# Another order of hand-placed items, and one cast of values on ScalarE instead of GpSimd

## The chip, the cores and the metric

The kernel runs on 1 core of one Trainium2 chip. Its engines are TensorE (PE, with the loading of stationary operands shown apart as PEld), VectorE (DVE), ScalarE (ACT), GpSimd (POOL) and SyncE (SP), which here only issues DMAs. The metric is the device time of one execution in microseconds; the median of several runs counts.

## The reference

Attention for 4 batches of 8 heads (768 rows, 64 wide), then a two-layer MLP with a prelu over the 3,072 rows that come out:

```python
scores = q @ k.T / 8                         # per batch and head
mask   = causal                              # heads 0, 2, 6 ("retrieval")
mask   = causal & (key < 4 | row - key < 64) # the other heads ("streaming")
a = softmax(where(mask, scores, -1e9))
x = a @ v                                    # 3072 x 512 over all heads
h = x @ w_in                                 # 512 -> 2048
g = maximum(h, 0) + alpha * minimum(h, 0)
out = g @ w_out                              # 2048 -> 512, float32
```

Inputs are float32 in DRAM; the kernel computes with bf16 operands.

## The kernel before

**Pairs.** A batch's eight heads are worked in four pairs: heads (2,6), (1,5), (0,4), (3,7). A pair has a number n = 4 * batch + place, from 0 to 15; "batch 1's first pair" is pair 4, the retrieval heads 2 and 6 of batch 1, and pair 5 holds two streaming heads.

**Items.** The whole program is cut into 1,112 named items, each a few instructions, and emitted in the order of a table of names written at the top of the file:

```python
for name in ORDER:
    if not beside_burst(name):
        emit_burst()
    I[name]()
```

Every engine executes its own instructions in that order; an instruction that waits holds up all behind it on the same engine. Waits between engines are put in by the framework. The names, with n a pair and t a tile of 256 or 512 rows:

- `Lq`, `Lk`, `Lv` load queries, keys, values of a pair as float32 (SP); `Cq`, `Ck`, `Cv` cast them to bf16 on an engine that the strings `CQ`, `CK`, `CV` name (V, A, P for DVE, ACT, POOL). `Cv` is L370, tile `vb<-raw`.
- `Tq`, `Tk` transpose on PE (L385), `tq`, `tk` copy the result out of PSUM (L390, L410 to L418).
- `S` scores (L447 or L454), `s` their exp on ACT (L493 for retrieval heads, into `eR`; L565 and L567 for streaming ones, into `eS`), `m` the mask, multiplied on DVE (L502 for `eR`, 128x128; L576 and L579 for `eS`).
- `An.h` the product with the values (L603), `an.h` its normalisation on DVE (L613, L614), which also gives its PSUM bank back; `Xn` a DMA that transposes the result into the MLP's input.
- `P`, `p`, `g` the first layer's matmuls (L649), its relu on ACT (L654) and the prelu on DVE (L661); `O`, `o` the second layer (L669) and its copy and store (L675, L679).
- For four of the eight tiles (t = 0, 2, 4, 7) the second layer is done with seven products instead of eight (Strassen's scheme): `W1` to `W4` subtract blocks of w_out from each other (L723, DVE, 128x2048), `Gt.x` add or subtract blocks of g (L728, DVE, 128x2048), `Mt.x.s` are the products (L741, PE, 8 matmuls of 256 columns each), `k` and `c` keep and combine them (L769, L776, L779 and others). For example, `M0.2` reads plain blocks of g and w_out, `M0.4` reads W4, which needs W1; `W2` also needs W1.

**Bursts of scores.** Score matmuls of pairs 4 and up are not emitted at their item: `S` collects them, and the next item that does not stand in the list of harmless ones (`beside_burst`) emits what has been collected, as one burst. If both heads have at least `SPLIT` = 576 columns in it, they are paired: each matmul uses 64 rows of the array and the two heads run side by side (L454); otherwise each uses the whole array, with zeros in the other half (L447).

```python
if min(columns) < SPLIT:
    for x in burst:
        nc.tensor.matmul(*x[3:6], start=True, stop=True)             # L447
else:
    ...
        nc.tensor.matmul(to, keys[own], queries[own], ...)           # L454
```

**Shape of the program.** Batch 0's attention comes first, then items of the attention of one batch are mixed with MLP items of the batch before. The attention of batch 1 (pairs 4 to 7) runs beside the MLP of batch 0; the first layer of batch 1's rows (tile 2, `P2.x`) begins at 80.85 us.

Of the kernel before, what the change touches and what calls it, by code (L numbers as in the profile page):

```python
# [32 lines left out]
near1 Cv4 tq7 Lk9 a5.1 Lk10 a5.0 Lq9 X5 Lk11 Cv7 m4.1.4 G0.1 G0.3 M0.1.0 M0.1.1 c0.00 G0.2 S6.1.0 S7.0.2 S6.0.3 S7.1.1
S6.0.1 S7.1.0 s6.1.0 s7.1.1 s7.1.0 A4.0 a4.0 m7.1.0 S6.0.5 s6.0.3 s6.0.1 m7.1.1 S6.0.0 O1.0.0 O1.0.1 S7.0.0 S6.1.2
s6.0.5 s6.0.0 m6.0.3 s7.0.2 m6.1.0 S6.1.1 m7.0.2 S7.1.2 m6.0.0 S6.0.4 s6.0.4 Lq8 Cv6 s6.1.1 A4.1 m6.1.1 M0.6.1 s7.1.2
S7.0.1 a4.1 s6.1.2 X4 s7.0.1 M0.6.0 m6.0.5 S6.0.2 s7.0.0 s6.0.2 m7.1.2 A7.1 k0.01 m6.1.2 m6.0.1 A6.1 m6.0.4 A6.0
m7.0.1 m7.0.0 A7.0 O1.0.2 O1.0.3 a6.1 a6.0 M0.5.0 M0.5.1 k0.11 a7.1 a7.0 W3 M0.7.1 M0.7.0 G0.4 M0.3.1 M0.3.0 c0.01 X6
X7 P2.2 Ck9 Cq9 Cq8 Lq10 P2.5 p2.5 g2.5 P2.8 p2.8 Lq11 P2.15 g2.8 p2.15 g2.15 p2.2 g2.2 P2.0 Dk8.0 Dk9.1 p2.0 g2.0
P2.6 p2.6 g2.6 c0.10 c0.11 Dk8.1 Dq8 Dk9.0 Lv10 P3.0 p3.0 P2.9 P2.4 p2.9 g2.9 g3.0 P3.12 p3.12 Dq9 Ck10 g3.12 P3.2
o1.0 p2.4 g2.4 p3.2 g3.2 Cq10 P2.14 p2.14 g2.14 P2.3 p2.3 g2.3 P2.10 p2.10 g2.10 P3.14 p3.14 g3.14 P2.7 p2.7 g2.7  # L40
P2.11 p2.11 g2.11 P2.13 Dq10 Lv8 P3.8 P3.6 p2.13 g2.13 S8.1.5 Lv11 S9.0.0 S8.1.4 p3.8 g3.8 p3.6 g3.6 S8.0.5 S8.0.1
P2.12 P3.10 Cq11 S9.1.1 s9.0.0 s8.0.5 m8.0.5 p2.12 s8.1.4 m8.1.4 m6.0.2 s9.1.1 s8.1.5 m9.0.0 m9.1.1 g2.12 Ck11 S8.0.3
s8.0.3 P2.1 p2.1 m8.1.5 Cv8 m8.0.3 p3.10 g3.10 S8.0.0 s8.0.0 P3.4 p3.4 g3.4 M2.4.0 M2.4.1 k2.10 s8.0.1 g2.1 Dk10.1
S10.1.0 m8.0.1 s10.1.0 m10.1.0 O3.0.0 O3.0.1 G2.1 G2.3 Lv9 Cv9 Dk11.0 Dq11 S9.1.0 S9.0.2 S9.0.1 S9.1.2 S10.1.2 S8.0.4
S8.1.1 s9.1.0 O3.0.2 O3.0.3 M2.2.0 M2.2.1 m8.0.0 Lq13 Lk13 s9.0.2 Dk10.0 Dk11.1 Cv10 s10.1.2 s9.0.1 S11.0.1 S11.0.0
S10.1.1 s8.0.4 s9.1.2 m9.1.2 o3.0 s8.1.1 S8.1.3 S11.0.2 s10.1.1 s8.1.3 m10.1.2 m9.0.2 m9.0.1 A9.0 k2.00 m9.1.0 A9.1
m8.0.4 m10.1.1 A10.1 M2.1.0 S8.0.2 a9.0 a9.1 s11.0.2 m11.0.2 s8.0.2 m8.1.3 X9 M2.1.1 s11.0.1 a10.1 s11.0.0 A8.0 G2.2
S10.0.1 S10.0.5 S8.1.0 S11.1.2 S10.0.2 M2.5.0 c2.00 M2.6.1 m8.1.1 s10.0.1 s11.1.2 m11.1.2 s8.1.0 S11.1.1 S10.0.3 Lq15
a8.0 S8.1.2 m11.0.0 s10.0.5 S11.1.0 S10.0.0 s10.0.2 S10.0.4 s8.1.2 Lv14 Lq12 m10.0.1 Cq13 m8.1.0 m10.0.5 s10.0.0 Cv11
Ck13 s10.0.4 m10.0.4 m11.0.1 m10.0.0 s10.0.3 m10.0.3 s11.1.0 s11.1.1 M2.5.1 A8.1 a8.1 m11.1.0 M2.6.0 A10.0 m11.1.1  # L50
a10.0 A11.0 Dk13.0 a11.0 k2.01 M2.7.0 A11.1 a11.1 k2.11 M2.7.1 G2.4 Cq12 X8 O3.1.0 O3.1.1 O3.1.2 O3.1.3 M2.3.1 M2.3.0
c2.10 c2.11 X10 X11 Lk12 P4.12 p4.12 c2.01 P5.14 P4.6 g4.12 P4.7 p4.7 g4.7 P4.8 p4.8 p5.14 g5.14 P5.10 p5.10 g5.10
g4.8 P5.0 p5.0 Ck12 Lq14 Dq12 g5.0 P5.12 p5.12 P5.2 P4.4 p4.4 p4.6 g4.4 g4.6 Cq14 Dk13.1 Cv14 P5.6 p5.6 p5.2 g5.2 o3.1
Dq13 g5.6 P5.4 P4.14 p4.14 g4.14 p5.4 g5.4 P4.1 p4.1 g4.1 P4.15 P4.3 p4.15 g4.15 g5.12 S13.1.0 s13.1.0 P4.10 P4.13
p4.13 g4.13 p4.10 g4.10 Lv15 Dk12.0 Dk12.1 P4.9 p4.9 g4.9 P4.5 p4.5 Lv12 Lk14 P4.2 p4.2 m12.0.2 g4.5 S12.0.1 g4.2
s12.0.1 P5.8 p5.8 O5.1.0 S12.1.1 g5.8 S13.1.1 p4.3 S12.0.0 g4.3 S12.0.5 S12.0.3 s12.0.3 O5.1.1 Lv13 Lk15 S12.1.5
s12.1.1 m12.1.1 Cv12 s12.1.5 S12.0.4 s12.0.4 P4.11 p4.11 m12.0.1 Dq14 Cq15 Ck14 m13.1.0 g4.11 s12.0.0 s12.0.5 m12.0.5
S12.0.2 s12.0.2 m12.0.4 m12.0.0 P4.0 p4.0 O5.1.2 O5.1.3 m12.0.3 A12.0 s13.1.1 m10.0.2 Dk14.0 Ck15 Cv13 o5.1 Dk14.1
S13.0.2 s13.0.2 O5.0.0 S13.0.0 S13.1.2 S13.0.1 g4.0 a12.0 S14.0.5 S12.1.2 O5.0.1 s13.1.2 G4.1 G4.3 S14.0.1 s14.0.5
S12.1.4 s13.0.0 m13.0.0 s13.0.1 s12.1.2 m13.0.1 S14.0.0 m13.1.2 S14.1.2 S14.1.0 s14.0.1 s14.1.0 m13.0.2 m14.1.0 O5.0.2  # L60
O5.0.3 S12.1.3 S12.1.0 S14.1.1 s14.0.0 s12.1.4 m12.1.4 s14.1.2 m14.1.2 m13.1.1 S14.0.2 S14.0.4 s14.0.4 s12.1.0 s12.1.3
o5.0 A13.0 M4.1.0 a13.0 Dk15.1 Dk15.0 A13.1 Dq15 m12.1.3 s14.0.2 a13.1 m14.0.5 Cv15 X13 m12.1.5 s14.1.1 m14.1.1 M4.5.0
M4.5.1 S14.0.3 S15.1.0 S15.0.2 S15.1.1 S15.1.2 m14.0.1 S15.0.1 s14.0.3 s15.1.2 s15.1.0 m14.0.4 M4.1.1 m14.0.3 m14.0.0
A14.1 A14.0 k4.0 m15.1.2 m12.1.0 A12.1 G4.2 M4.6.0 a14.0 s15.0.1 S15.0.0 M4.2.0 a14.1 X14 s15.0.2 m15.1.0 s15.1.1
m15.1.1 A15.1 M4.6.1 m15.0.2 s15.0.0 m15.0.0 m15.0.1 A15.0 a12.1 M4.2.1 k4.1 a15.1 a15.0 G4.4 M4.7.0 M4.7.1 k4.2
M4.3.1 M4.3.0 c4.11 M4.4.0 M4.4.1 X12 c4.10 X15 P7.4 P7.12 c4.01 P7.10 P7.0 p7.10 g7.10 p7.0 g7.0 P7.1 p7.1 g7.1 P7.9
P7.7 p7.7 g7.7 P7.3 p7.3 g7.3 p7.12 g7.12 P7.6 P7.13 p7.9 g7.9 P7.2 p7.2 g7.2 P7.14 p7.6 g7.6 p7.4 P6.4 P7.15 p7.14
g7.14 P6.0 p7.15 g7.15 p7.13 G7.3a P7.5 P6.6 p7.5 g7.5 g7.13 g7.4 G7.1b G7.2b P7.11 p7.11 g7.11 p6.6 P6.14 p6.0 g6.0
p6.14 M7.1.0 P7.8 p7.8 g6.14 g7.8 M7.1.1 p6.4 k7.0 g6.6 P6.10 P6.12 p6.10 G7.1a g6.10 P6.2 M7.2.0 P6.8 p6.8 M7.2.1
M7.5.0 M7.5.1 k7.2 c4.00 G7.2a M7.6.0 G7.4a M7.6.1 G7.4b M7.3.1 p6.12 g6.12 p6.2 g6.2 M7.3.0 g6.4 k7.1 g6.8 c7.01  # L70
O6.0.0 O6.0.1 O6.0.2 G7.3b M7.7.1 M7.7.0 c7.11 c7.00 d7.0 O6.0.3 L2 o6.0 l2 M7.4.1 M7.4.0 L1 l1 c7.10 d7.1 L0 l0
""".split()


# [1 line left out]
def kernel(  # L76
# [291 lines left out]
    def cast_v(n):  # L368
        vv = vb[n % NV]
        cast_of(CV[n])(vv[:, :, :, 0:D], vf[n % NF])  # L370
# [651 lines left out]
```

## Time and profile before

| | us |
|---|---|
| median of 3 runs | 224.33 |
| the three runs | 224.09, 224.33, 225.03 |
| profiled execution, its time | 224.55 |
| its span in the trace | 222.8 |
| PE busy | 214.1 (96%) |
| DVE busy | 181.7 (82%) |
| ACT busy | 142.3 (64%) |
| POOL busy | 44.8 (20%) |
| granted TensorE clock, mean | 0.999 |

The time of the profiled execution is longer than its span by what lies before the first and behind the last recorded instruction. A row of the timeline gives the start, the length from the first start to the last end, engine, line, operation, output and inputs, and how many instructions were joined; in brackets stand the idle time ahead and what ended it. A matmul's end is modelled, so where matmuls follow each other without a stop, the difference of two starts says more than a length. In a table of windows the columns behind the window are its length and the busy time of PE, PEld, DVE, ACT and POOL with their counts, then the clock, the share of DMA and its GB/s.

### The profile page before, as it was taken

What the parts mean: (1) busy time and instruction counts of PE and PEld (TensorE: products, weight loads), DVE (VectorE), ACT (ScalarE), POOL (GpSimd) and SP (SyncE); (2) the same over time, 40 slices, a digit from 0 to 9 for tenths busy, and PEclk for the clock granted to TensorE, in tenths of its full rate; (3) what the DMA queues carried; (4) which work ended last, traced back from release to release, by engine and by line L of the source; (5) the groups of instructions that cost most, each with busy time, mean ns of one, the idle gap of its engine ahead of it and who ended that gap; (6) DMA issues with size and microseconds to landing.
All of it is one profiled execution on the core that took longest, in us unless ns stands there. A gap on an engine that the chain in (4) does not pass through costs nothing.

```text
span 222.8 us, 5570 instructions
## 1 busy us (share of the span) xinstructions
PE 214.1 (96%) x2131; PEld 153.1 (69%) x2151; DVE 181.7 (82%) x441; ACT 142.3 (64%) x289; POOL 44.8 (20%) x88
## 2 busy tenths in 40 slices
...
GB/s 201 320 245 218 269 214 289 195 196 241 196 249 242 94 197 191 203 229 176 220 129 266 147 282 175 206 207 70 190 101 42 118 96 1 0 0 50 0 150 137
DMA packets 96155, 37.61 MB, mean 169 GB/s; under 512 B 83176, under 2 KB 94336, under 8 KB 96128
## 3 DMA queue, kind: packets, MB, share of 16 engines
q1 hardware_dynamic: 89600, 27.39, 57.8%
...
q8 instruction: 17, 0.28, 0.5%
q14 instruction: 10, 0.08, 0.1%
...
## 4 chain that ended last, share of the span: by engine, by line
PE 72%; DVE 8%; DMA 8%; SPq 5%; issue 3%; POOL 2%; ACT 0%; DVEq 0%; POOLq 0%
PE P L649 33%; PE P L741 20%; PE P L669 9%; DMA raw<-in_k_dram 8%; PE P L603 5%; PE P L454 3%; SPq L236 2%; DVE g L661 2%; PE P L688 2%; PE P L447 1%; SPq L220 1%; DVE eR L502 1%; DVE g L728 1%; DVE ws L723 1%; POOL w_in_b L835 1%
## 5 line engine op out<-in xcount | busy, mean ns | idle before, releaser
L649 PE MATMUL P<-xT,w_in_b 128*128 128x256 bf16 (+1 forms) x501 | 86.7, 325 | 0.7 <-issue 0.2
L661 DVE SCALAR_TENSOR_TENSOR g<-neg,oma,P 128x256 bf16<-128x256 f32 (+1 forms) x128 | 70.9, 608 | 17.1 <-ACT neg L654 16.3
L654 ACT ACTIVATE neg<-P 128x512 f32<-128x512 f32 x96 | 55.0, 602 | 35.9 <-PE P L649 27.2
L649 PEld LDWEIGHTS <-w_in_b 128*128 128x128 bf16 x512 | 49.5, 98 | 30.9 <-issue 0.2
L493 ACT ACTIVATE eR<-P 128x448 bf16<-128x448 f32 (+3 forms) x63 | 35.6, 623 | 6.8 <-PE P L454 2.9
L741 PEld LDWEIGHTS <-g 128*128 128x128 bf16 x368 | 34.8, 98 | 6.0 <-issue 0.4
L669 PE MATMUL P<-w_out_b,g 128*128 128x512 bf16 x103 | 25.4, 379 | 0.4
L741 PE MATMUL P<-ws,g 128*128 128x256 bf16 x192 | 23.4, 273 | 0.2 <-DVE ws L723 0.2
L565 ACT ACTIVATE eS<-P 128x352 bf16<-128x352 f32 x45 | 20.6, 481 | 4.0 <-PE P L454 2.6
L741 PE MATMUL P<-w_out_b,g 128*128 128x256 bf16 x176 | 21.8, 273 | 0.0
L614 DVE TENSOR_TENSOR xn<-P,rcp 128x448 bf16<-128x448 f32 (+1 forms) x32 | 19.0, 595 | 1.1
L669 PEld LDWEIGHTS <-g 128*128 128x128 bf16 x112 | 10.3, 98 | 10.8 <-DVE g L661 0.7
L679 POOL DMA_DIRECT2D out_dram<-ot x6 | 3.4, 562 | 55.8 <-ACT ot L675 50.1
L576 DVE TENSOR_TENSOR eS<-eS,ms_near 128x352 bf16<-128x352 bf16 x45 | 14.2, 335 | 0.1
L779 POOL DMA_DIRECT2D out_dram<-ot x8 | 5.9, 738 | 39.5 <-DVE ot L776 33.5
L728 DVE TENSOR_TENSOR g<-g 128x2048 bf16<-128x2048 bf16 x10 | 12.8, 1280 | 0.1
L502 DVE TENSOR_TENSOR eR<-eR,mr_near 128x128 bf16<-128x128 bf16 x54 | 10.9, 233 | 0.7 <-ACT eR L493 0.6
L603 PE MATMUL P<-vb,eS 128*128 128x65 bf16 x266 | 11.0, 193 | 0.3 <-DVE vb L327 0.2
L603 PEld LDWEIGHTS <-eS 128*128 128x128 bf16 x266 | 10.0, 97 | 1.8 <-issue 0.6
L447 PE MATMUL P<-qT,kT 128*128 128x176 bf16 (+7 forms) x66 | 10.1, 256 | 0.0
...
L603 PE MATMUL P<-vb,eR 128*128 128x65 bf16 x258 | 9.6, 192 | 0.1
...
## 6 DMA issues: line engine op xcount, KB each, us to landing
...
```

What stands on the lines that cost most here:

```text
L493: nc.scalar.activation(ebuf[n, hh][:, lo:hi].rearrange("p (x c) -> p x c", x=len(parts)), P[:, got[0]:got[0] + len(parts), 0:(hi - lo) // ...
L502: nc.vector.tensor_tensor(ej, ej, mr_near, op=ALU.mult)
L565: nc.scalar.activation(slots, sc[:, 0:352].rearrange("p (s c) -> p s c", c=176), AF.Exp, scale=scale)
L576: nc.vector.tensor_tensor(slots, slots, ms_near[:, 0:2, :] if m == 0 else ms_near[:, 1:3, :], op=ALU.mult)
L603: nc.tensor.matmul(pav[:, i, :], e[:, o:o + 128], vv[:, j, hh, 0:D + 1], start=(m == 0), stop=(m == len(terms) - 1))
L614: nc.vector.tensor_tensor(xn[n][:, 0:nt, D * hh:D * hh + D], pav[:, :, 0:D], rcp.to_broadcast([128, nt, D]), op=ALU.mult)
L649: nc.tensor.matmul(psg[:, w * i:w * (i + 1)], w_in_b[:, c, 128 * fb:128 * (fb + 1)], xT[:, c, o:o + w], start=(x == 0), stop=(x == 3))
L654: nc.scalar.activation(neg[t, f], bank(held["P", t, f][0]), AF.Relu, scale=-1.0)
L661: nc.vector.scalar_tensor_tensor(g_buf[TOK[t][1]][:, fb, 0:w], neg[t, f][:, c], oma[:, fb:fb + 1], bank(got[0])[:, c], op0=ALU.mult, op1=A ...
L669: nc.tensor.matmul(bank(held["O", t, s][0]), g_buf[TOK[t][1]][:, f, 128 * s:128 * (s + 1)], w_out_b[:, f, :], start=(f == 0), stop=(f == 15))
L728: nc.vector.tensor_tensor(G_SUM[t][x - 1][:, c, :], a[:, c, :], b[:, c, :], op=ALU.add if x == 1 else ALU.subtract)
L741: nc.tensor.matmul(bank(held[to, t][0])[:, 256 * s:256 * s + 256], g[:, f, 128 * s:128 * (s + 1)], w[:, f, :], start=(first and f == 0), s ...
```

## The change

Two things change, and nothing else. One letter in the string that names the engine for each pair's cast of values:

```diff
-    CV = "PPPPPPVVVVVVVVVV"
+    CV = "PPPPAPVVVVVVVVVV"
```

So `Cv4` runs on ACT; `Cv5` stays on POOL. And the table of items behind the first 310 (of 1,112) holds the same names in a new order. Its first lines:

```diff
-S5.0.1 p1.10 s5.0.1 P1.6 S4.1.4 m4.0.1 s4.0.3 near0 g1.10 S4.1.3 p1.12 S4.0.5 s4.0.5 m5.1.1 S4.0.4 s4.0.4 g1.12 m4.0.3
+S5.0.1 p1.10 s5.0.1 p1.12 S4.0.0 m4.0.1 g1.10 P1.6 S4.0.2 S4.0.5 S4.1.4 s4.0.3 g1.12 s4.0.0 m4.0.0 O1.1.0 near0 m5.0.2
...
```

What this does to the queues is seen in the instructions of an engine, one row each; `waits` names the engine or DMA queue whose semaphore is waited for. On PE, around the first product with pair 5's values (`A5.1`), before (`g_87` and `g_86` are the activations of 256-row and of 512-row tiles, `natm_84` the keys of pair 7, `vb` the cast values; repeated pairs of rows are left out):

```order
L385 MATMUL P<-ident,natm_84 128x128 [waits Activation_49]
...
L669 LDWEIGHTS g_87
L669 MATMUL P<-w_out_b,g_87 128x512 [waits DMASW2_49]
...
L741 LDWEIGHTS g_86
L741 MATMUL P<-w_out_b,g_86 128x256 [waits Activation_49]
...
L741 MATMUL P<-w_out_b,g_86 128x256 [waits DMASW3_49]
...
L603 LDWEIGHTS eS [waits Activation_49]
L603 MATMUL P<-vb,eS 128x65 [waits Pool_49]
```

and after:

```order
L669 MATMUL P<-w_out_b,g_87 128x512 [waits DMASW2_49]
...
L447 MATMUL P<-qT,kT 128x320
L385 LDWEIGHTS natm_84
L385 MATMUL P<-ident,natm_84 128x128 [waits Activation_49]
...
L603 LDWEIGHTS eS [waits Activation_49]
L603 MATMUL P<-vb,eS 128x65 [waits Pool_49]
...
L741 LDWEIGHTS g_86
L741 MATMUL P<-w_out_b,g_86 128x256 [waits DVE_49]
```

The sixteen L741 (`M0.2.0`, `M0.2.1`) stood ahead of `A5.1`, whose L603 waits for POOL's cast; now they stand behind it.

On DVE at the same place, around the weight sums `W2` and `W4` (the two L723 with `ws` as an input), before:

```order
L502 TENSOR_TENSOR eR<-eR,mr_near 128x128
L304 MEMSET eR 128x64
L502 TENSOR_TENSOR eR<-eR,mr_near 128x128 [waits Activation_49]
L502 TENSOR_TENSOR eR<-eR,mr_near 128x128 x2
L723 TENSOR_TENSOR ws<-w_out_b,ws 128x2048 [waits DMASW3_49,DMASW2_49,DVE_49]
L723 TENSOR_TENSOR ws<-w_out_b,ws 128x2048 [waits DVE_49]
L355 CAST natk_81<-raw 128x2x7x64 [waits DMAHW3_49,DMAHW2_49]
```

and after:

```order
L502 TENSOR_TENSOR eR<-eR,mr_near 128x128 [waits Activation_49] x2
L502 TENSOR_TENSOR eR<-eR,mr_near 128x128
L723 TENSOR_TENSOR ws<-w_out_b,ws 128x2048 [waits DMASW3_49,DMASW2_49,DVE_49]
L502 TENSOR_TENSOR eR<-eR,mr_near 128x128 [waits Activation_49]
L723 TENSOR_TENSOR ws<-w_out_b,ws 128x2048 [waits DVE_49]
L613 RECIPROCAL rcp<-P 128x7 [waits PE_49]
L614 TENSOR_TENSOR xn<-P,rcp 128x7x64 [waits DVE_49]
```

A mask now stands between the two sums, and a normalisation comes ahead of the cast of keys that followed them.

On ACT, where the moved cast lands, before:

```order
L336 CAST natq_80<-raw 128x2x6x64 [waits DMAHW1_49]
L769 COPY ot<-P 128x512 [waits PE_49]
L675 COPY ot<-P 128x512 [waits PE_49]
L390 COPY qT<-P 128x768 [waits PE_49]
L565 ACTIVATE eS<-P 128x2x176 [waits DVE_49,PE_49]
```

and after:

```order
L336 CAST natq_80<-raw 128x2x6x64 [waits DMAHW1_49]
L769 COPY ot<-P 128x512 [waits DVE_49,PE_49]
L675 COPY ot<-P 128x512
L370 CAST vb<-raw 128x14x64 [waits DMAHW7_49,DMAHW0_49]
L390 COPY qT<-P 128x768 [waits PE_49]
L565 ACTIVATE eS<-P 128x2x176 [waits DVE_49,PE_49]
```

`Cv4` (L370) stands between the copy of an MLP result and the copy of pair 7's transposed queries, and one `k` copy (L769) has moved behind the exp. The order of DMAs on SyncE's queue is the same row by row in both programs. The number of matmuls is the same too; how the score matmuls fall into bursts is not, and nine of them move from L447 to L454.

More of the change, by code (lines that the diff above doesn't have):

```diff
@@ L28 @@
 Lv6 S4.0.1 Cq6 m12.1.2 P0.5.0 s4.0.1 P0.5.1 P0.5.2 P1.12 m5.0.0 g1.4 S4.0.3 g0.7 p0.4 p0.5 m5.1.0 g0.4 g0.5 Cv5 P1.10
-S5.0.1 p1.10 s5.0.1 P1.6 S4.1.4 m4.0.1 s4.0.3 near0 g1.10 S4.1.3 p1.12 S4.0.5 s4.0.5 m5.1.1 S4.0.4 s4.0.4 g1.12 m4.0.3
-S4.0.0 m5.0.2 Tq6 S4.1.0 O1.1.0 p1.6 g1.6 O1.1.1 m4.0.5 p0.6 s4.1.4 g0.6 s4.0.0 s4.1.0 m5.0.1 S4.1.1 W1 s4.1.3 S4.0.2
-s4.0.2 m4.1.3 S4.1.5 s4.1.5 S4.1.2 m4.1.5 S5.1.2 s5.1.2 m5.1.2 s4.1.1 Tk6 tk6.1 m4.0.0 tk6.0 Tk7 O1.1.2 s4.1.2 tk7.1
-Lv4 ro1 m4.1.1 tq6 tk7.0 Cq7 M0.2.0 M0.2.1 k0.00 m4.0.4 A5.1 O1.1.3 o1.1 A5.0 m4.1.0 W2 W4 Ck8 M0.4.0 M0.4.1 k0.10 Tq7
@@ L33 @@
[L33 to L71, printed above, removed]
+S5.0.1 p1.10 s5.0.1 p1.12 S4.0.0 m4.0.1 g1.10 P1.6 S4.0.2 S4.0.5 S4.1.4 s4.0.3 g1.12 s4.0.0 m4.0.0 O1.1.0 near0 m5.0.2
@@ new lines @@
+p1.6 g1.6 S5.1.2 s4.0.5 s5.1.2 p0.6 S4.1.5 s4.1.5 O1.1.1 Tq6 s4.1.4 S4.1.3 m5.0.1 S4.1.0 s4.1.0 s4.1.3 Tk6 m5.1.1
+m4.0.5 S4.1.1 s4.1.1 tk6.1 m5.1.2 O1.1.2 W1 g0.6 S4.0.4 tk6.0 Tk7 s4.0.4 tk7.1 A5.1 Lv4 ro1 m4.0.3 m4.1.5 s4.0.2
+m4.1.0 m4.1.3 M0.2.0 m4.1.4 A5.0 tq6 tk7.0 Cq7 W2 m4.1.1 O1.1.3 M0.2.1 k0.00 W4 M0.4.0 M0.4.1 a5.1 Ck8 Tq7 near1
+m6.0.2 o1.1 a5.0 Cv4 tq7 Lk9 Lk10 Lq9 X5 S6.1.0 s6.1.0 m4.0.4 M0.1.0 M0.1.1 G0.1 k0.10 S7.0.0 S7.1.2 S7.0.2 S7.1.0
+S6.0.3 G0.3 G0.2 O1.0.0 s7.0.0 m7.0.0 c0.00 s7.1.0 S4.1.2 s7.1.2 m7.1.2 s7.0.2 A4.0 s6.0.3 m6.1.0 S6.0.5 a4.0 s6.0.5
@@ new lines @@
+m6.0.5 Lk11 Cv7 Lq8 Cv6 m7.1.0 S6.0.2 s6.0.2 O1.0.1 s4.1.2 S6.0.1 S6.1.1 m7.0.2 S7.1.1 S6.0.0 S6.1.2 s7.1.1 m7.1.1
+m6.0.3 s6.1.2 M0.6.0 s6.0.0 m6.1.2 m6.0.0 s6.0.1 s6.1.1 m6.1.1 S6.0.4 m6.0.1 M0.6.1 s6.0.4 S7.0.1 m6.0.4 A4.1 a4.1
+s7.0.1 m7.0.1 A6.1 a6.1 A6.0 a6.0 A7.1 a7.1 A7.0 a7.0 O1.0.2 M0.5.0 M0.5.1 G0.4 O1.0.3 k0.11 M0.3.0 k0.01 M0.3.1 W3
+M0.7.0 X4 X6 M0.7.1 X7 P2.7 P2.15 c0.01 P2.8 p2.15 P3.2 p2.8 Ck9 Cq9 Cq8 Lq10 Lq11 p2.7 c0.10 c0.11 P2.6 g2.7 Dk8.0
+g2.8 g2.15 p2.6 P3.12 p3.12 g3.12 Dk9.1 P3.8 p3.8 g2.6 g3.8 P2.14 p2.14 g2.14 P2.13 p2.13 g2.13 P2.11 p3.2 g3.2 p2.11
@@ new lines @@
+Dk8.1 o1.0 P2.5 P2.4 Dq8 Dk9.0 p2.5 g2.11 Lv10 g2.5 Dq9 Ck10 Cq10 Dq10 p2.4 P3.14 p3.14 g2.4 P3.0 P3.6 p3.0 g3.0 g3.14
+Lv8 p3.6 P2.0 p2.0 g2.0 g3.6 P2.3 p2.3 g2.3 P2.2 P2.10 p2.2 g2.2 P2.9 p2.10 g2.10 p2.9 S8.1.5 g2.9 S8.0.1 S9.0.0
+S8.0.5 S8.1.4 s8.1.4 P2.1 s8.0.1 m8.0.1 Lv11 Cq11 Ck11 p2.1 P2.12 g2.1 s9.0.0 p2.12 g2.12 s8.0.5 m8.0.5 s8.1.5 m8.1.5
+P3.10 p3.10 g3.10 P3.4 p3.4 g3.4 S9.1.0 S9.1.1 S8.0.0 S8.0.3 S9.1.2 Cv8 s9.1.2 m9.0.0 M2.4.0 M2.4.1 s9.1.1 s8.0.0
+O3.0.0 m9.1.1 k2.10 G2.1 m8.0.0 G2.3 O3.0.1 Dk10.1 S9.0.1 s8.0.3 S8.0.2 S9.0.2 S8.0.4 S10.1.2 s9.1.0 m9.1.0 S10.1.0
```

27 lines of the change are left out of this document (added).

## Prediction

> **What bounds the kernel now.** I read the page first (parts 1 and 4), then the busy time by stage, then where TensorE stops inside the one stage in which it does, and last the other engines around those stops.
>
> ```profile
> PE 214.1 (96%) x2131; PEld 153.1 (69%) x2151; DVE 181.7 (82%) x441; ACT 142.3 (64%) x289; POOL 44.8 (20%) x88
> PE 72%; DVE 8%; DMA 8%; SPq 5%; issue 3%; POOL 2%; ACT 0%; DVEq 0%; POOLq 0%
> 0.00:49.00 49.00, 46.40 (x542) 34.90 (x547) 39.75 (x105) 39.70 (x67) 29.33 (x66) 1.00 1.08 239
> ```
>
> The first line is busy time by engine, the second the chain that ended last, the third the first 49 us: length, then busy time of PE, PEld, DVE, ACT and POOL. TensorE (PE) is the bound. The order differs only behind the first 310 items, about 49 us in, so the 2.6 us that PE idles before that stay. The rest, in the same columns:
>
> ```profile
> 49.21:80.85 31.64, 30.31 (x358) 23.17 (x360) 28.88 (x80) 22.74 (x54) 3.39 (x4) 1.00 0.94 205
> 80.85:216.00 135.15, 134.43 (x1203) 92.52 (x1213) 112.58 (x256) 78.86 (x166) 12.13 (x18) 1.00 0.63 134
> ```
>
> From 80.85 us, where batch 2's first-layer matmuls begin, PE is busy 134.43 of 135.15 us: no wait there is worth a gain, and only the length of PE's own work counts. From 49.21 to 80.85 it idles 1.33 us. The release of these stops is in PE's timeline (start, length, what, and in brackets the idle time before and its releaser):
>
> ```profile
> 54.96 0.83 PE L385 MATMUL P<-ident,natm 128*128 128x128 bf16 x12
> 55.63 1.03 PE L669 MATMUL P<-w_out_b,g 128*128 128x512 bf16 x4
> 56.49 1.91 PE L741 MATMUL P<-w_out_b,g 128*128 128x256 bf16 x16
> 58.24 0.55 PE L603 MATMUL P<-vb,eS 128*128 128x65 bf16 x13
> 58.85 0.81 PE L669 MATMUL P<-w_out_b,g 128*128 128x512 bf16 x3
> 60.29 1.92 PE L741 MATMUL P<-ws,g 128*128 128x256 bf16 x16 [0.23 <-DVE ws L723]
> 68.61 0.72 PE L454 MATMUL P<-qT,kT 64*128 64x176 bf16 x12 [0.61 <-DVE xn L614]
> 58.24:80.85 22.61, 21.55 (x283) 17.05 (x284) 19.84 (x49) 13.79 (x34) 2.45 (x3) 1.00 0.89 199
> ```
>
> Two stops have a named releaser: 0.23 us for the last sum of second-layer weights (W4, L723), 0.61 us for a normalisation (L614) that gives a PSUM bank back. Behind 58.24 PE idles 1.06 us in all. L603 at 58.24 is A5.1, the first product that reads the values of pair 5, which GpSimd casts:
>
> ```profile
> 56.69 0.94 POOL L370 CAST vb<-raw 128x896 bf16<-128x896 f32 x1 [13.43 <-DMA raw<-in_v_dram]
> 63.88 1.18 POOL L370 CAST vb<-raw 128x896 bf16<-128x896 f32 x1
> 56.63 1.21 DVE L502 TENSOR_TENSOR eR<-eR,mr_near 128x128 bf16<-128x128 bf16 x3
> 57.76 2.47 DVE L723 TENSOR_TENSOR ws<-w_out_b,ws 128x2048 bf16<-128x2048 bf16 x2
> 63.04 3.09 DVE L728 TENSOR_TENSOR g<-g 128x2048 bf16<-128x2048 bf16 x2
> 49.21:56.49 7.28, 7.00 (x61) 4.55 (x60) 7.28 (x27) 7.23 (x17) 0.00 (x0) 1.00 1.19 237
> L502 DVE TENSOR_TENSOR eR<-eR,mr_near x54: 179/219/980, 49.9 to 167.3; 128x128 bf16<-128x128 bf16 x54
> L728 DVE TENSOR_TENSOR g<-g x10: 1208/1218/1833, 63.0 to 173.5; 128x2048 bf16<-128x2048 bf16 x10
> ```
>
> The first row is the cast of pair 5 (Cv5), released by the landing of its values and ended at 57.63; the second that of pair 4 (Cv4). Each froze a DVE instruction beside it (the last two rows: shortest, median and longest in ns): a mask that takes 219 ns took 980, until Cv5 ended, and a sum of activations took 1833 instead of 1218 beside Cv4. Cv4 itself, 1.18 against 0.94, first stood behind the sum before.
>
> **The change part by part.** *The order around A5.1.* In the program of before, the four L669 at 55.63 are followed by two Strassen products (M0.2.0 and M0.2.1, the L741 at 56.49, 58.24 - 56.49 = 1.75 us), and A5.1 comes behind them, 0.61 us after its cast. In the new order A5.1 stands straight behind the transposes of L385, and both products behind it. What stands ahead of it is otherwise what stood ahead of M0.2.0, less one score matmul of 448 columns (0.19 us at the rate below): PE arrives at 56.49 - 0.19 = 56.30, or at 56.0 if the 7.28 - 7.00 = 0.28 us that it idles between 49.21 and 56.49 go as well. The cast cannot start before its load lands (SyncE's queue of loads is the same row by row), so A5.1 has to wait for Cv5's end.
>
> When is that? Who is first at it, Cv5 or the sum W2, decides. DVE is busy without a gap ahead of W2 (7.28 of 7.28 us between 49.21 and 56.49), so W2 starts when the work ahead of it is done; compared kind by kind, the new order has the same work ahead of W2 less one mask of L502. Before, W2 started at 57.76 with a mask frozen for 0.980 - 0.219 = 0.76; without a freeze it would have been 57.0, and without one mask (0.14 to 0.22 of DVE's time) 56.8. Ahead of W2 stand five masks in a row. So Cv5 at 56.69 finds single masks of 0.2 us beside it, waits at most the rest of one, and freezes the next: Cv5 56.7 to 57.65 again, W2 at about 57.7. I take 57.70 for A5.1, a wait of 57.70 - 56.30 = 1.40 us (1.70 from 56.0). Masks and W2 thus still meet this GpSimd cast, by a margin of about 0.1 us; only Cv4 is taken away from the sums.
>
> *What PE does from there.* The work from A5.1 to 80.85 is 21.55 us busy, to which come the products that A5.1 overtook (1.75) and the score matmul moved behind it (0.19): 57.70 + 23.49 = 81.19, if no stop is left and nothing else is saved. The 0.23 goes: A5.1, A5.0 and the L669 between took 60.29 - 58.24 - 0.23 = 1.82 and the products 1.75, so PE reaches M0.4.0, which reads W4, at 57.70 + 3.57 = 61.27; W4 is done at 57.76 + 2.47 = 60.23 or a little earlier. The 0.61 goes: its normalisation follows G0.3, no longer frozen (1.833 - 1.218 = 0.61 us earlier on DVE), and PE comes later. After a stop the rows count about 0.1 us of fill as busy, so 21.3 to 21.55 is the work; I take 81.05, i.e. +0.20, before the savings of the next part.
>
> *Paired score matmuls.* Scores of two heads run either on the whole array (L447) or side by side on halves of it (L454), the latter only when both heads of a burst have at least 576 columns. What is in a burst depends on the order of items: counted in the two programs, L447 goes from 66 matmuls with 14,368 columns to 57 with 11,776, L454 from 138 with 27,104 to 147 with 29,696. 2,592 columns move, in one burst more.
>
> ```profile
> 109.39 1.75 PE P L741 x16
> 115.65 0.68 PE P L454 x9
> 116.33 1.85 PE P L741 x16
> ```
>
> These are pieces of the chain. 16 x 256 columns in 1.75 us are 0.427 ns a column; two heads at once save half of 2,592, 1,296 x 0.427 = 0.55 us. A paired burst costs something at its ends: the one at 115.65 has a longer half of 1,344 columns, 0.57 us at that rate, and took 0.68, and the product behind it took 1.85 instead of 1.75, so 0.21 us. Net -0.34 us. From below zero to above: -0.55 (free ends) to +0.2 (PE waits for masks or exps of the larger burst and only the ends remain). I take -0.35, which is what the chain shows for such a burst.
>
> *Cv4 on ScalarE.*
>
> ```profile
> 61.22 0.84 ACT L336 CAST natq<-raw 128x768 bf16<-128x768 f32 x1
> 62.43 0.59 ACT L675 COPY ot<-P 128x512 f32<-128x512 f32 x1
> 63.39 0.82 ACT L390 COPY qT<-P 128x768 bf16<-128x768 bf16 x1
> 64.67 1.18 ACT L565 ACTIVATE eS<-P 128x352 bf16<-128x352 f32 x3 [0.47 <-PE P L454]
> ```
>
> No cast of 896 elements on ScalarE is in the trace; the nearest is 768 elements in 0.84 us, so 0.84 x 896/768 = 0.98. It stands between L675 and L390, and delays L390 and the exps by at most 0.98 us; 0.47 of it lies in the idle time before the L565 that waits for PE, and the scores it waits for come about as late as PE is (+0.2). What is left, some 0.3 us, would show only where PE waits for an exp, and none of its stops behind 58.24 has an exp (an L493 or L565) as its releaser. I take 0; if that cover is gone, +0.3. On the other side Cv4 is done at about 63.4 instead of 65.06, for an A4.0 that did not wait for it, and DVE gets 0.61 us back that is off PE's path once the 0.61 stop is gone: 0 as well.
>
> The **Trainium skill**, "SBUF — State Buffer", section "Who interferes with whom", calls the port pair of DVE and GpSimd an exclusive lock: whoever issues first holds it for the whole instruction, the other is blocked, and ScalarE never takes part. By that rule Cv4's cost to DVE vanishes, as I have it. The same rule speaks against the new place of W2, which is the first rival. The trace agrees so far with 0.980 and 1.833 us for frozen DVE instructions and 1.18 for a cast that came second.
>
> **Sum.** Up to 80.85 +0.20, then -0.35 for the bursts: -0.15 on the profiled execution's 224.55 (span 222.8): 224.4. That execution stands 0.22 above the median of 224.33, so on the median 224.33 - 0.15 = 224.2.
>
> **The rivals.**
> 1. *The cast comes second (slower).* W2 could now start at about 56.8. If pair 5's values land 0.15 to 0.2 us later, or the masks end as much earlier, W2 (1.23 us) is first at the port and Cv5 runs from about 58.05 to 59.0: A5.1 at 59.07 instead of 57.70, +1.37 us that nothing behind it gives back: 224.2 + 1.37 = 225.6. For it: Cv4's 1.18, a cast that had to wait. Against it: the start of 56.69 is set by a load whose queue does not change, and the mask that it freezes stands ahead of W2. Decided by Cv5's start before or after W2's.
> 2. *The values land earlier (faster).* With Cv5 done by 56.3, the wait of 1.40 is gone and PE would be at 80.85 - 1.2: but the 0.61 stop comes back, since PE comes earlier and DVE does not. About -0.8: 223.4; if the stop stays away as well, 222.8. Against it: nothing in SyncE's order moves, and the load's transfer goes when it did.
> 3. *Paired bursts bring nothing.* The larger burst makes the exps and masks behind it later, and PE stops between two products. Then +0.20 + 0.2, 224.7.
> 4. *The change does not do what it says.* This is part of my forecast: Cv5 stays on GpSimd beside masks and W2; only Cv4's meeting with G0.3 ends.
>
> **How the numbers follow.** Two medians of three runs of this kernel differ by up to about 0.5% (its runs go from 224.09 to 225.03), 1.12 us: 223.2 to 225.45 is "same". The forecast, 224.2 with a range of its own of 223.8 to 224.7, has 0.56; rival 1 at 225.6 has 0.20, rival 2 at 222.8 to 223.4 0.10, rival 3 at 224.7 0.14. The forecast and rival 3 are "same" (0.70); of rival 2 four fifths end below 223.2 (0.08), of rival 1 about two thirds above 225.45 (0.13), the rest of both "same" (0.09). I move 0.02 from same to faster for stops elsewhere in these 32 us. Low 223.0 and high 225.6 leave out about a tenth at each end.
>
> **What would show it.** Right: PE's waits list A5.1 (L603 released by the cast L370 on GpSimd) with about 1.4 us, its thirteen L603 start at 57.7, the POOL cast is there once, at 56.7; a mask of L502 again takes near 1 us, no L728 takes 1.8; W2 starts at about 57.8; the second-layer waits of 0.23 and 0.61 are gone; batch 2's L649 start at 81.0 or a little earlier, with L454 x147 and L447 x57. Wrong: Cv5 starting after W2 (rival 1), L603 at 56.3 without a wait (rival 2), or stops of PE behind 81 us, above all in front of an L603 that follows a paired burst (rival 3). An end that is off by more than 0.3 us from these with all steps seen would mean that the work of PE itself was counted wrongly.

## The result and the profile after

| | us |
|---|---|
| median of 20 runs, before | 224.38 |
| median of 20 runs, after | 223.33 |
| ratio after to before, 95% interval | 0.994 (0.9916 to 0.9964) |
| profiled execution after, its time and span | 222.47, 220.7 |

The changed kernel is 0.6% faster by the ratio and 0.5% by the medians; 223.33 lies just inside what I had called "same" (223.2 to 225.45), the forecast was 224.2, the range 223.0 to 225.6. Ratios here and below leave out runs more than 1.5% above the fastest of the same kernel (six disturbed ones of 279 to 1258 us among them), while medians count every run, so that where a kernel's runs lie far apart the median says more: for the late load below the ratio keeps four of twelve runs, for the change once more nine.

First the page's busy times of the changed kernel, then its stretch up to batch 2's first layer in the columns of the windows:

```profile
PE 214.0 (97%) x2130; PEld 153.8 (70%) x2151; DVE 180.2 (82%) x441; ACT 142.7 (65%) x290; POOL 44.6 (20%) x87
49.21:80.85 31.64, 30.85 (x359) 23.34 (x363) 30.13 (x84) 22.91 (x55) 3.72 (x4) 1.00 1.00 204
```

PE's work is the same, 214.0 us against 214.1. In the same window PE idles 0.79 us instead of 1.33, and part of the window is already the next stage, as PE's timeline shows:

```profile
49.03 1.04 PE L649 MATMUL P<-xT,w_in_b 128*128 128x256 bf16 x8
55.89 0.55 PE L603 MATMUL P<-vb,eS 128*128 128x65 bf16 x13
56.28 1.04 PE L741 MATMUL P<-w_out_b,g 128*128 128x256 bf16 x8
61.38 0.51 PE L385 MATMUL P<-ident,natq 128*128 128x128 bf16 x6 [0.16 <-ACT natq L336]
79.75 2.54 PE L649 MATMUL P<-xT,w_in_b 128*128 128x512 bf16 x10
```

A5.1 (L603 at 55.89) stands without a wait, the stops of 0.23 and 0.61 us are gone, and batch 2's first layer begins at 79.75 instead of 80.85. Counted from the eight L649 that stood at 49.21 before and stand at 49.03 now, this stage takes 30.72 us instead of 31.64. The other engines at that place:

```profile
54.24 1.59 POOL L370 CAST vb<-raw 128x896 bf16<-128x896 f32 x1 [12.22 <-DMA raw<-in_v_dram]
53.83 1.21 DVE L723 TENSOR_TENSOR ws<-w_out_b 128x2048 bf16<-128x2048 bf16 x1
55.70 0.89 DVE L502 TENSOR_TENSOR eR<-eR,mr_near 128x128 bf16<-128x128 bf16 x6
56.51 1.21 DVE L723 TENSOR_TENSOR ws<-w_out_b,ws 128x2048 bf16<-128x2048 bf16 x1
61.27 3.81 DVE L728 TENSOR_TENSOR g<-g 128x2048 bf16<-128x2048 bf16 x3
62.17 0.96 ACT L370 CAST vb<-raw 128x896 bf16<-128x896 f32 x1
```

Pair 5's values landed at 54.24 in this execution, not at 56.69. Cv5 met W1 (L723 at 53.83) instead of masks, and it was the cast that waited: 1.59 us instead of 0.94, done at 55.83. So six masks run in 0.89 us, W2 starts at 56.51 instead of 57.76, and three sums of activations take 3.81 us, unfrozen.

Behind it, the last copy of the result (ACT, L697) in before and after:

```profile
218.79 0.37 ACT L697 COPY ot<-P 128x256 f32<-128x256 f32 x1 [2.05 <-PE P L688]
```

```profile
217.38 0.37 ACT L697 COPY ot<-P 128x256 f32<-128x256 f32 x1 [1.75 <-PE P L688]
```

From the first layer's start to this copy it is 137.94 us before and 137.63 after. From the copy to the end of the span it is 4.01 and 3.32. The 2.1 us by which this execution is shorter are 0.18 ahead of 49 us, 0.92 in the stage, 0.31 behind it and 0.7 in the last store. Which of these belong to the change, and which to this execution?

### The profile page after: what moved, and what is told of

It is laid out like the page before. It is cut to its first block, busy times and chain, and to the rows that moved or that the text cites. A ratio compares the mean times of both kernels' runs of the same rounds, so it can differ in the third digit from the quotient of the medians.

```text
span 220.7 us, 5567 instructions
## 1 busy us (share of the span) xinstructions
PE 214.0 (97%) x2130; PEld 153.8 (70%) x2151; DVE 180.2 (82%) x441; ACT 142.7 (65%) x290; POOL 44.6 (20%) x87
## 3 DMA queue, kind: packets, MB, share of 16 engines
HBM read 27.71 MB, written 6.29 MB: 154 GB/s over the span
## 4 chain that ended last, share of the span: by engine, by line
PE 83%; DVE 8%; ACT 2%; DMA 2%; issue 1%; SPq 1%; POOL 0%; DVEq 0%
PE P L649 36%; PE P L741 20%; PE P L669 10%; PE P L603 7%; PE P L454 4%; DVE g L661 3%; DMA raw<-in_q_dram 2%; PE P L688 2%; PE P L385 2%; DVE ws L723 2%; PE P L437 1%; PE P L447 1%; PE P L628 1%; DVE eR L502 1%; DVE kT L410 1%
## 5 line engine op out<-in xcount | busy, mean ns | idle before, releaser
L649 PE MATMUL P<-xT,w_in_b 128*128 128x256 bf16 (+1 forms) x498 | 86.1, 324 | 0.8 <-issue 0.2
L649 PEld LDWEIGHTS <-w_in_b 128*128 128x128 bf16 x512 | 49.4, 98 | 30.7 <-issue 0.2
L741 PEld LDWEIGHTS <-g 128*128 128x128 bf16 x368 | 34.8, 98 | 6.3 <-DVE g L728 0.3
L669 PE MATMUL P<-w_out_b,g 128*128 128x512 bf16 x105 | 26.4, 380 | 0.5 <-DVE g L661 0.2
L741 PE MATMUL P<-ws,g 128*128 128x256 bf16 x192 | 23.6, 273 | 0.0
L741 PE MATMUL P<-w_out_b,g 128*128 128x256 bf16 x176 | 21.7, 273 | 0.0
L728 DVE TENSOR_TENSOR g<-g 128x2048 bf16<-128x2048 bf16 x10 | 12.2, 1219 | 0.2
L603 PE MATMUL P<-vb,eS 128*128 128x65 bf16 x266 | 11.0, 193 | 0.1
L603 PEld LDWEIGHTS <-eS 128*128 128x128 bf16 x266 | 9.8, 97 | 1.5 <-issue 0.5
L603 PE MATMUL P<-vb,eR 128*128 128x65 bf16 x258 | 9.8, 193 | 0.0
L454 PE MATMUL P<-qT,kT 64*128 64x176 bf16 (+7 forms) x147 | 9.5, 249 | 0.1
L502 DVE TENSOR_TENSOR eR<-eR,mr_near 128x128 bf16<-128x128 bf16 x54 | 9.5, 216 | 0.1
```

The source lines that it names most:

```text
L454: nc.tensor.matmul(to, keys[own], queries[own], start=True, stop=True)
L603: nc.tensor.matmul(pav[:, i, :], e[:, o:o + 128], vv[:, j, hh, 0:D + 1], start=(m == 0), stop=(m == len(terms) - 1))
L649: nc.tensor.matmul(psg[:, w * i:w * (i + 1)], w_in_b[:, c, 128 * fb:128 * (fb + 1)], xT[:, c, o:o + w], start=(x == 0), stop=(x == 3))
L669: nc.tensor.matmul(bank(held["O", t, s][0]), g_buf[TOK[t][1]][:, f, 128 * s:128 * (s + 1)], w_out_b[:, f, :], start=(f == 0), stop=(f == 15))
L728: nc.vector.tensor_tensor(G_SUM[t][x - 1][:, c, :], a[:, c, :], b[:, c, :], op=ALU.add if x == 1 else ALU.subtract)
L741: nc.tensor.matmul(bank(held[to, t][0])[:, 256 * s:256 * s + 256], g[:, f, 128 * s:128 * (s + 1)], w[:, f, :], start=(first and f == 0), s ...
```

## Experiments

Theory A: the order makes the gain, by the stops in the stage up to 80 us and the additional paired burst behind it. Theory B: the values happened to land early in the one profile after, and the order has no part in it. Theory C: the cast's move makes the gain.

**The parts alone.** The first experiment is the old order with the cast moved.

```diff
-    CV = "PPPPPPVVVVVVVVVV"
+    CV = "PPPPAPVVVVVVVVVV"     # ORDER as before
```

> The old order, with only the cast of pair 4's values (Cv4) moved from GpSimd to ScalarE. If the order makes the gain: within 0.3 us of before, first-layer matmuls of batch 2 (P2) at 80.85 us less what Cv5's landing moves, the stop ahead of the scores at 68.6 smaller by up to 0.6 because G0.3 takes 1.2 us instead of 1.8. If the cast makes it: 0.6 to 0.9 us faster, with P2 at about 80.0.

Median 224.2 us, ratio 0.9994 (0.9968 to 1.002): nothing. Its PE and ACT show why:

```profile
63.58 0.96 ACT L370 CAST vb<-raw 128x896 bf16<-128x896 f32 x1
64.42 0.81 ACT L390 COPY qT<-P 128x768 bf16<-128x768 bf16 x1
65.28 0.74 PE L454 MATMUL P<-qT,kT 64*128 64x176 bf16 x13 [0.71 <-ACT qT L390]
81.01 1.24 PE L649 MATMUL P<-xT,w_in_b 128*128 128x512 bf16 x5
```

The stop at 68.6 is gone, but one of the same size, 0.71 us, stands at 65.28: the old order has the whole burst of scores behind the copy of pair 7's queries (L390), which the cast now delays. The stop has only changed its reason. C alone falls.

The second is the new order with `CV` as before.

```diff
-    CV = "PPPPAPVVVVVVVVVV"
+    CV = "PPPPPPVVVVVVVVVV"     # ORDER as after
```

> The new order, with Cv4 still on GpSimd. If the order makes the gain: 0.8 to 1.3 us faster than before, as the full change, P2 at about 79.8 when pair 5's values land near 54 us. If the cast makes it: 0 to 0.4 us faster, a sum of activations (L728) of 1.8 us again, and a stop of PE of up to 0.6 us behind it.

Median 224.87, ratio 1.0007 (0.9972 to 1.0043): nothing either, although the values landed early:

```profile
54.68 1.40 POOL L370 CAST vb<-raw 128x896 bf16<-128x896 f32 x1 [11.57 <-DMA raw<-in_v_dram]
57.33 1.23 DVE L723 TENSOR_TENSOR ws<-w_out_b,ws 128x2048 bf16<-128x2048 bf16 x1 [0.50 <-DMA w_out_b<-in_moe_w_out_dram]
62.11 4.65 DVE L728 TENSOR_TENSOR g<-g 128x2048 bf16<-128x2048 bf16 x3
63.39 0.95 POOL L370 CAST vb<-raw 128x896 bf16<-128x896 f32 x1
68.98 0.50 PE L454 MATMUL P<-qT,kT 64*128 64x176 bf16 x6 [0.97 <-DVE xn L614]
81.02 1.24 PE L649 MATMUL P<-xT,w_in_b 128*128 128x512 bf16 x5
```

With Cv4 on GpSimd the three sums take 4.65 us instead of 3.81, and PE stops for 0.97 us for the normalisation behind them. The stage is 31.74 us (from 49.28), 1.02 longer than in the profile of the full change. Not all of the 0.97 is the cast's: here W2 also waited 0.50 us for its weights (L723 at 57.33), which put the sums back. With unfrozen sums the stop would have been 0.97 - 0.84 = 0.13 us, without the wait for the weights 0.47. So the two parts need each other: the cast's move frees DVE, and only the new order has work for PE beside the cast on ACT.

**The front and the back.** Two hybrids cut the table at the first `P2` item: the new one's front (with `CV` of after) and the old one's rest, and the reverse.

```diff
 # e3: ORDER of after up to the first P2 item, then the remaining items in the order of before
 # e4: ORDER of before up to the first P2 item, then the remaining items in the order of after; CV of before
```

> The full change up to batch 2's first-layer matmuls, the old order behind them. If the stops between 49 and 81 us make most of the gain: 0.6 to 1.0 us faster than before. If the paired score matmuls behind make it: 0 to 0.3 faster. If it is only that the values landed early in the profiled execution: no difference to before on the median, and P2's start moves with Cv5's start from one kernel's profile to the next.

> The old order up to batch 2's first-layer matmuls, the new order behind them, Cv4 on GpSimd. If the stops between 49 and 81 us make most of the gain: 0.3 us faster than before, from the extra burst of paired score matmuls; the way from P2's start to the last second-layer matmul is 0.3 shorter than in before. If the back makes it all: 0.8 to 1.2 us faster.

The new front gives 223.8, ratio 0.999 (0.9955 to 1.0025); the new back 223.78, ratio 0.996 (0.9933 to 0.9987). For the front, the profile caught what I had forecast for the full change:

```profile
55.82 1.01 POOL L370 CAST vb<-raw 128x896 bf16<-128x896 f32 x1 [13.88 <-DMA raw<-in_v_dram]
56.89 0.55 PE L603 MATMUL P<-vb,eS 128*128 128x65 bf16 x13 [1.12 <-POOL vb L370]
80.30 1.89 PE L649 MATMUL P<-xT,w_in_b 128*128 128x512 bf16 x8
```

Cv5 ends at 56.83, A5.1 waits 1.12 us for it, and the first layer begins 23.41 us behind A5.1. The stage is 31.34 (from 48.96): between before's 31.64 and the 30.72 of the early landing. The twelve runs fall into two groups, seven from 222.88 to 223.99 and five from 225.14 to 226.5, and the cast alone, with the old front, has no such gap in its runs (223.56 to 225.35). What makes the upper group is not shown: none of the five was profiled, and only one has a lowered clock (0.989). For the new back:

```profile
81.11 1.24 PE L649 MATMUL P<-xT,w_in_b 128*128 128x512 bf16 x5
218.75 0.37 ACT L697 COPY ot<-P 128x256 f32<-128x256 f32 x1 [1.75 <-PE P L688]
```

137.64 us to the last copy, as in the full change (137.63); the new front with the old back takes 137.93, as before (137.94). The back is worth 0.30 us to that copy, whatever stands ahead. The runs do not divide the gain between front and back so clearly: by the ratios the new back alone is 0.4% faster and the new front alone is not clear of no change; by the medians (223.78 and 223.8, against 224.43 of before beside them) the two are alike. The order alone (1.0007) holds this back too, so its front without the cast's move loses about what the back gains.

**The landing moved on purpose.** These three experiments, and the products ahead below, ran on another chip than those above, beside runs of before with a median of 224.53. SyncE's queue was changed by one place of `Lv5`, the load of pair 5's values:

```diff
-... Lq6 Lv7 ... Lv5 ... Lq7 ...
+... Lq6 Lv5 Lv7 ... Lq7 ...      # e5 in the new order, e6 in the old one
+... Lq6 Lv7 ... Lq7 Lv5 ...      # e7, new order
```

> The full change, with the load of pair 5's values (Lv5) issued ahead of pair 7's (Lv7) instead of behind it. If the spread of the new order comes from A5.1 waiting for Cv5: Cv5 starts before 54 us, A5.1 stands near 55.9 without a wait in every execution, P2 starts at about 79.7, the runs lie closer together, and the median is 0.3 to 0.9 us below that of the full change (about 222.4 to 223.0, 0.65 to 0.9% below before). If Cv5's landing is not what sets the median: as the full change, 0.6% below before, with the same spread.

> The kernel before, with Lv5 ahead of Lv7. If the old order does not depend on Cv5's landing (A5.1 stands 1.75 us later there): within 0.3 us of before, P2 at 80.7 to 81.0, the stop of 0.6 us ahead of the scores at 68.6 still there. If the early landing alone explains the gain seen in the profile after: 0.8 to 1.1 us faster than before, P2 near 79.9.

> The full change, with Lv5 issued behind the load of pair 7's queries (Lq7), so that the values land 1 to 3 us later. If A5.1 waits for Cv5: a wait of PE for the cast L370 of 1.5 to 4 us, A5.1 at Cv5's end plus 0.06 us, P2 23.4 us behind it, and, where Cv5 starts behind W2, Cv5 delayed by up to 1.2 us more; 1 to 3 us slower than the full change. If the wait is hidden: no slower than 0.3 us.

In the new order, values early: 222.75, ratio 0.9929 (0.9895 to 0.9963), runs from 222.31 to 224.66, and a stage of 80.04 - 49.31 = 30.73 us with no wait for the cast, which starts at 44.73. In the old order, values early (Cv5 at 49.36): 224.3, ratio 0.9973 (0.9942 to 1.0004); its stage is 80.80 - 49.35 = 31.45, 0.2 shorter, and a stop of 0.50 us for the normalisation stays. So an early landing in the old order does not give what the full change gives: theory B falls, though the landing has a part in it.

```profile
44.73 1.30 POOL L370 CAST vb<-raw 128x896 bf16<-128x896 f32 x1 [1.55 <-DMA raw<-in_v_dram]
80.04 2.32 PE L649 MATMUL P<-xT,w_in_b 128*128 128x512 bf16 x10
```

```profile
68.56 0.72 PE L454 MATMUL P<-qT,kT 64*128 64x176 bf16 x12 [0.50 <-DVE xn L614]
```

The first two rows are the new order's, the third is the old one's.

The late load is the dearest experiment: the median is 226.61, 2.08 us above before (ratio 0.9972, 0.9913 to 1.003, from four runs). POOL, DVE and PE of its profile, then windows of 1 us with PE's granted clock in the column behind the five busy times:

```profile
57.57 1.41 POOL L370 CAST vb<-raw 128x896 bf16<-128x896 f32 x1 [15.41 <-DMA raw<-in_v_dram]
56.96 1.23 DVE L723 TENSOR_TENSOR ws<-w_out_b,ws 128x2048 bf16<-128x2048 bf16 x1 [0.35 <-DMA w_out_b<-in_moe_w_out_dram]
59.03 0.88 PE L603 MATMUL P<-vb,eS 128*128 128x65 bf16 x13 [3.10 <-POOL vb L370]
85.27 9.91 PE L649 MATMUL P<-xT,w_in_b 128*128 128x512 bf16 x57
57.00:58.00 1.00, 0.00 (x0) 0.00 (x0) 1.00 (x1) 0.97 (x3) 0.43 (x1) 1.00 0.40 88
58.00:59.00 1.00, 0.00 (x0) 0.00 (x0) 1.00 (x3) 0.99 (x4) 0.98 (x1) 0.55 1.05 239
63.00:64.00 1.00, 1.00 (x4) 0.43 (x3) 0.43 (x2) 0.00 (x0) 0.00 (x0) 0.50 0.89 204
64.00:65.00 1.00, 1.00 (x7) 0.71 (x5) 0.00 (x0) 0.00 (x0) 0.00 (x0) 0.53 1.09 247
65.00:66.00 1.00, 1.00 (x11) 0.90 (x10) 0.00 (x0) 0.56 (x2) 0.00 (x0) 1.00 1.16 262
```

This is the first rival as the prediction drew it: W2 is first at the port, the cast waits it out (1.41 us, done at 58.98), A5.1 stands at 59.03. And then comes what no theory had: during the stop of 3.10 us PE's granted clock falls to 0.50, and it stays there until about 64.9. The first layer begins 26.24 us behind A5.1 instead of 23.41: 2.83 more, about half of the 5.9 us from 59.03 to 64.9. The Trainium skill, "TensorE: Matmul & The Clock Gate", section "Part 1: The HAM clock gate", gives the array's clock a half and a full state, chosen by how busy it was, with a free-running window of about 3.4 us; the 0.50 here agrees with the half.

Nine of these twelve executions show a mean clock of at most 0.992. Of the kernels with A5.1 in its new place and the load in its old one, 6 of 56 executions do (1 of 20 of the full change, 2 of 12 in its repetition, 2 of 12 with the order alone, 1 of 12 with the new front); of the kernels with the old front, or with the products back or the load ahead, 1 of 84 does, a disturbed run of 370 us.

**The wait covered.** On PE alone the two products M0.2 are put back ahead of A5.1, first with the load as it is, then together with the early and the late load.

```diff
-Tk7 s4.0.4 tk7.1 A5.1 Lv4 ... m4.1.3 M0.2.0 m4.1.4 A5.0 ... O1.1.3 M0.2.1 k0.00
+Tk7 s4.0.4 tk7.1 M0.2.0 M0.2.1 A5.1 Lv4 ... m4.1.3 m4.1.4 A5.0 ... O1.1.3 k0.00
```

> The full change with one piece put back: on PE both products M0.2 stand ahead of A5.1 and A5.0 again, the other engines' orders are the same. If the wait at A5.1 costs in the executions in which the values land late: no wait for L370 up to a landing of 57 us, P2 at about 79.7 to 79.9, fewer runs above 224, median 0.2 to 0.6 us below the full change. If the products then wait instead (for the last quarter of w_out or for a PSUM bank): the same median as the full change, with a new wait at L741.

> The full change with both remedies: Lv5 issued ahead of Lv7, and the products M0.2 ahead of A5.1. If each only takes away the same wait: no better than one of them, 0.6 to 0.8% below before, with no wait for L370. If something else still spreads the new order (the landing of w_out or of the queries): the same median, and the waits named there. Faster than 222.4 only if the two took away different waits.

> The late load (Lv5 behind Lq7) with the products M0.2 ahead of A5.1. With the late load alone PE stopped for 3.1 us and the granted clock fell to 0.5 for 6.6 us. If that stop is what cost: PE now has 1.75 us of products in it, the wait for L370 is at most 1.4 us, the clock stays at 1.0, and the median is 223 to 224, 2.5 to 3.5 us below the late load alone. If the clock fell for another reason than the stop: it falls again, and the median stays above 226.

Products ahead: 223.21, ratio 0.9936 (0.9904 to 0.9968), with Cv5 at 57.27, the latest of all profiles with the load in its old place, no wait for L370, and a stage of 30.98; a stop of 0.48 us for W4 (L723) is back. Both remedies: 223.12, ratio 0.9947 (0.9921 to 0.9972), stage 30.72: no better than one, as expected if both take away the same wait. With the late load and the products ahead:

```profile
56.51 0.97 POOL L370 CAST vb<-raw 128x896 bf16<-128x896 f32 x1 [13.50 <-DMA raw<-in_v_dram]
58.13 0.95 PE L603 MATMUL P<-vb,eS 128*128 128x65 bf16 x26
56.00:60.00 4.00, 3.94 (x55) 2.99 (x52) 4.00 (x11) 3.93 (x11) 0.97 (x1) 1.00 0.72 163
```

In this profile the values landed a little earlier than in the late one above, so it alone proves little; the runs do. No stop, a clock of 1.00, median 223.28 (ratio 0.9959, 0.9936 to 0.9982), the twelve runs within 222.61 and 224.05: 3.33 us below the late load alone, in the expected 2.5 to 3.5. The two ran on different chips; counted from before on its own chip, the late load is 2.08 us slower and this kernel 0.86 faster (224.14 to 223.28), 2.94 us apart. It was the stop that cost.

**The change once more**, on the chip of the last two (both remedies, and the late load with the products ahead):

> The full change as it is, beside the next two on the same chip, for another look at where pair 5's values land. If the landing decides: Cv5 starts between 54 and 57 us; A5.1 at 55.9 or at Cv5's end plus 0.06 us, whichever is later, P2 23.4 to 23.9 us behind A5.1, the last copy (L697, 256 columns) 137.63 behind P2. Median about 0.6% below before.

```profile
55.98 0.98 POOL L370 CAST vb<-raw 128x896 bf16<-128x896 f32 x1 [14.34 <-DMA raw<-in_v_dram]
56.02 1.57 DVE L502 TENSOR_TENSOR eR<-eR,mr_near 128x128 bf16<-128x128 bf16 x6
57.02 0.55 PE L603 MATMUL P<-vb,eS 128*128 128x65 bf16 x13 [0.85 <-POOL vb L370]
80.43 1.89 PE L649 MATMUL P<-xT,w_in_b 128*128 128x512 bf16 x8
```

Median 223.81, against 224.14 of before beside it: 0.15%, not the expected 0.6; the ratio, from nine runs, is 0.9947 (0.991 to 0.9983), and all twelve go from 221.91 to 226.87. A wait of 0.85, and again exactly 23.41 us from A5.1 to the first layer; the stage is 31.07. This execution shows the chain that the prediction drew: the cast freezes a mask (six masks take 1.57 us instead of 0.89), and A5.1 waits for its end.

**The price of pairing.** All bursts unpaired:

```diff
-    SPLIT = 576
+    SPLIT = 9576
```

> The full change with SPLIT raised so that no burst of scores is paired: all score matmuls use the whole array. The thirteen paired bursts of the full change have 12,672 columns in their shorter halves. At 0.427 ns a column these save 5.41 us, less 13 x 0.21 us for their ends: 2.7 us, so this kernel is 2.7 us longer, 1.7 of it behind P2's start. If the ends cost nothing: 5.4 longer. If the pairing saves nothing: within 0.5 us.

```profile
81.80 17.49 PE L649 MATMUL P<-xT,w_in_b 128*128 128x512 bf16 x104
221.68 0.37 ACT L697 COPY ot<-P 128x256 f32<-128x256 f32 x1 [1.75 <-PE P L688]
L447 PE MATMUL P<-qT,kT x204: 192/239/353, 37.7 to 173.0; 128*128 128x176 bf16 x45, 128*128 128x128 bf16 x14, 128*128 128x448 bf16 x12, 128*128 128x64 bf16 x7
```

One run, 226.82 us. From the first layer to the last copy it takes 139.88 us, 2.25 longer than paired; the front's two bursts add about 0.4 (31.12 from 50.68, against 30.72). Together 2.65, against 2.7 expected. The share of 1.7 for the back, in the expectation, was a slip: the eleven bursts there have 10,976 of the 12,672 columns, so the same formula says 10,976 x 0.427 = 4.69, less 11 x 0.21, = 2.38. Backwards, 4.69 - 2.25 = 2.44 us for eleven bursts: 0.22 us for the ends of one.

## Why the prediction was right, and where not

The measured median lies in the range, but 0.9 us below the forecast and below the forecast's own 223.8 to 224.7. It lies in the second rival's 222.8 to 223.4, which had a chance of 0.10, and the profile after showed that rival's sign: L603 without a wait. That the range holds the result is in part luck.

- *The landing was a constant, and is not.* This is the step that failed. I took 56.69 us for Cv5's start because SyncE's queue does not change. In nine profiles with that queue unchanged it starts between 54.24 and 57.27 us. The spread is already there where SyncE issues the load. The last issue of Lv5, in before and then in after:

```profile
42.82 3.20 SPq L255 DMA_DIRECT2D raw<-in_v_dram  x1
```

```profile
40.77 2.79 SPq L255 DMA_DIRECT2D raw<-in_v_dram  x1
```

It ends at 46.02 and 43.56 us, and both casts start 10.7 us later. In seven of the nine profiles the cast starts 10.2 to 10.8 us behind that end; in the two others the issue ended as late as 50.08 and 53.08, and the cast starts 5.7 and 2.9 behind it. Lv5 stands ahead of the first item that the change moves, so the early landing is not the order's doing. In the profile after it was early, A5.1 stood at 55.89 instead of 57.70, and the forecast of +0.20 for this stage became -0.92. With landings of 55.82 and 55.98 the wait is there, 1.12 and 0.85 us instead of the 1.40 for 56.69.
- *From A5.1 to the first layer* I had 23.35 (with 81.05) to 23.49 us; two profiles with the wait gave 23.41. The form "Cv5's end plus 0.06, plus 23.4" holds, and the old stops are gone as said. With before's landing it gives 57.63 + 0.06 + 23.41 = 81.10, which is +0.25 where I had +0.20: the working was right, its input was not.
- *Cv4's move was costed at 0.* Wrong by 0.5 to 0.8 us: without it, the sums are frozen for 0.84 us (4.65 against 3.81) and PE stops for 0.97, of which up to 0.50 goes with the late weights of that profile. I had put the freed DVE time "off PE's path" because the stop of 0.61 would be gone; it is gone only because of the cast's move. The cost on ScalarE (0.96 measured, 0.98 worked out) is hidden in the new order, and is a stop of 0.71 in the old one, where I had said at most 0.3.
- *Paired bursts*: -0.35 was forecast. The back alone gives -0.30, and the ends of a burst cost 0.22 against my 0.21. But I counted half of the moved columns, 1,296. What a paired burst saves is its shorter half, and these grow from 11,488 to 12,672 columns in the two programs, by 1,184: 0.51 us, less 0.21, is 0.30.
- *A tail that the sum left out.* From the last copy to the span's end it is 3.24 to 3.84 us in ten profiles with the new back (mean 3.46) and 3.67 to 4.01 in four with the old one (mean 3.85), another 0.4. In the new order the first of the last big stores is issued at 211.09 instead of 213.96, which is 6.29 us ahead of the last copy instead of 4.83. Whether this is the cause was not tried.
- *The first rival* (the cast second at the port) was given 0.20. It is real: forced with the late load, it put A5.1 at 59.03, where I had 59.07. But its price was too low, since the clock falls as well. That some executions of the unaltered change lose in the same way is likely from their lowered clocks (3 of 32), but none of them was profiled.
- *The sums and masks* "still meet this cast": yes, but in the profile after it was the cast that waited for W1.

Together: 0.3 to 0.9 us in the stage (31.34 with the new front, 31.07 and 30.72 with the change, against 31.64), 0.30 behind it and about 0.4 in the tail are 1.0 to 1.6, less some executions that land late; the ratio of 0.994 is 1.35, the medians differ by 1.05. Why SyncE's issues, and with them the landing, move by 3 us stays open; so does which of the three versions (the change, values early, products ahead) is the fastest, since their ratios of 0.9929 to 0.9947 overlap. By these ratios each is faster than before. By the medians values early (0.8%), products ahead (0.6%) and both (0.5%) are too; the change itself has 0.5% the first time and 0.15% the second.
